# Attention and mixture of experts on one core: the first expert's products ahead of the last turns, a copy ahead of a relu, the last y on two engines

## The chip, the cores and the metric

The kernel runs on one core of one Trainium2 chip. The metric is the device time of one execution in microseconds. The core has five engines with queues of their own: TensorE (PE; its weight loads are PEld in the profile), VectorE (DVE), ScalarE (ACT), GpSimd (POOL) and SyncE (SP), which here issues most of the transfers. Matmul results stand in PSUM banks of 128 x 512 f32, everything else on the chip in SBUF.

## The reference

Causal attention with a decay for 8 batches of 8 heads (576 tokens, 64 columns per head), whose output is the input of a mixture of 8 experts with one expert per token:

```python
scores = scale * np.matmul(q, k.transpose(0, 1, 3, 2))
cum = np.cumsum(np.log(np.clip(f, 0.0001, 1.0)), axis=-1)
scores = np.where(causal, -1e9, scores + cum[:, :, :, None] - cum[:, :, None, :])
attn = softmax(scores)
x = np.matmul(attn, v)                      # 4608 tokens x 512
expert_idx = np.argmax(x @ w_gate, axis=1)  # and gate_w, its softmax value
for e in range(8):
    h = np.maximum(x[expert_idx == e] @ w1[e], 0.0)    # 512 -> 1024
    out[expert_idx == e] = gate_w * (h @ w2[e])        # 1024 -> 512
```

## The kernel before, in words

**Attention.** A loop of 34 steps handles 32 head pairs (4 per batch), each step in seven parts i = 0 to 6. In step n TensorE computes pair n's scores, VectorE adds the mask and finds the row minima (line 421), ScalarE takes the exponentials (line 428); the same step turns (transposes) pair n - 1's scores on TensorE into PSUM (line 477), ScalarE and VectorE copy them out to aT (lines 473 and 471), and in part 1 TensorE multiplies pair n - 2's turned scores with v (line 553), whose results ScalarE copies to xT (line 561). sc_03, sc_13, sc_02 and so on are the pieces of a pair's scores by head and block of rows, sc_J is the joint piece of the last 64 rows of both heads. In step 32 no scores are left to compute: only the last pair's turns, the products of pair 30, and the tasks of the batch before the last.

**Operands in two parts.** A float32 operand of a product is kept as two parts: the rounded value (a cast on ScalarE) and the rest (a subtraction on VectorE or GpSimd). Each product is done as three: first part by first part, second by first, first by second.

**The first expert starts early.** Its first 384 tokens (chunk 0, CA = 384) are taken from batches that were ready before: three blocks of 128 tokens are fetched, turned by TensorE (`turn`, line 1129), cast by ScalarE (line 1134) and completed by VectorE (line 1135, called `end` in `early_tasks`); together they are the tile xa. `up(0, 0, ft)` computes hidden block ft (of 8): for each of four blocks of w1 (kt) three products with all 384 columns of xa into one PSUM bank of the pool ps_s (three banks), then a relu on ScalarE and a rest on VectorE. `extra` calls up(0, 0, 0) to up(0, 0, 4) in parts 2 to 6 of step 32, behind the tasks of that part. Of w1's four blocks, block 1 is cast last, in part 0 of step 32 (the cast named w<-y).

**Order.** `order.pin()` keeps each engine's instructions of the attention and the first expert in the order in which the program writes them.

**Experts 1 to 7.** The first layer is computed by a scheme of seven block products in place of eight (`seven`, called four times per expert with i = 0 to 3): seven groups of six products (s = 0 to 6) into four banks a, b, g, d. Banks a, b and g are used twice: the second use (s = 4, 5, 6) adds to the first, so the copies p1 (of a, line 1422) and p5 (of g, line 1428) have to be taken in between. GpSimd adds into p5 (line 1435). A relu and a rest (line 1413 and 1416) of each of the four results follow; three of them are left for the next call, in the list `self.ends`, whose entries the next call takes in s = 0 and s = 1.

**The second layer** (`down`) sums 24 products per 128 tokens into a bank; ScalarE scales them by the gate value to y (line 1201) and GpSimd scatters y to the output (line 1202). After the last expert stands `overflow`, a loop for experts with more than 640 tokens; with these inputs its loop does not run, but the instructions ahead of it (ov_ex, ov_cm and so on) do.

Of the kernel before, what the change touches and what calls it, by code (L numbers as in the profile page):

```python
# [13 lines left out]
AF = mybir.ActivationFunctionType  # L14
ALU = mybir.AluOpType
# [4 lines left out]
P = 128  # L20
# [3 lines left out]
D = H * HD  # L24
# [17 lines left out]
HN = CAP // 2  # L42
XM = 2 * (KT // 2) * HN
XN = ("T2", "T1", "T4", "T3", "B22")


class Ctx:
# [112 lines left out]
def psum(pool):  # L160
    return pool.tile([P, 512], F32, name="ps", tag="ps")
# [10 lines left out]
    tc.nc.gpsimd.tensor_copy(c.identr, c.ident)  # L172


def attention_all(c, tc, qkT, va, vb, f, wgd, x_dram, batch_done, more_consts, extra):

# [12 lines left out]
    with ExitStack() as st:  # L191
# [534 lines left out]
        for n in range(NP + 2):  # L726
# [11 lines left out]
            for i in range(7):  # L738
# [36 lines left out]
                    step(s_)  # L775
                for f in among.pop((n, i), []):
                    step(f)
                if ts_:
                    step(ts_[i])

# [14 lines left out]
                        todo = fin_tasks(fb)  # L795

                fin_bank[0] = (ps_v, ps_m)[i % 2]
                for f in tasks.pop((n, i), []):
                    step(f)
                at = {(0, 1): 0, (1, 0): 1, (1, 1 if b == B else 4): 2}.get((p, i))  # L800
# [1 line left out]
                    fin_sums(b - 1, at)  # L802
                if (n, i) == (NP, 0):
                    scores.close()
                for f in extra(n, i):
                    step(f)
                order.pin()
                if (n, i) == (NP + 1, 1):
                    break
# [233 lines left out]
class Moe:  # L1043
    def __init__(self, c, tc, x_dram, w1, w2, out):
        self.c, self.tc, self.nc = c, tc, tc.nc
        self.x_dram, self.w1, self.w2, self.out = x_dram, w1, w2, out
        self.w1p, self.w2p, self.xg, self.x, self.h = {}, {}, {}, {}, {}
        self.idx, self.w1raw, self.w2raw, self.py = {}, {}, {}, {}

        self.ups = 5  # L1050

    def split(self, raw, w):
        self.nc.scalar.copy(w[:, 0], raw)
# [90 lines left out]
    def begin_h(self, e, chunk):  # L1144
# [4 lines left out]
            c.words["hl", chunk].rearrange("p (f n) -> p f n", n=n),  # L1149
        )  # L1150

    def up(self, e, chunk, ft):

        c, nc = self.c, self.nc
        x = self.x[e, chunk]
        hh, hl = self.h[e, chunk]
        n = (CA, CB)[chunk]
        fs = slice(ft * P, ft * P + P)
        ph = psum(c.ps_s)
        k = 0  # L1160
        for kt in range(KT):
            w = self.w1p[e, kt]
            for wi, xi in ((0, 0), (1, 0), (0, 1)):
                c.note(nc.tensor.matmul(  # L1164
                    ph[:, 0:n], w[:, wi, fs], x[xi][:, kt, :],
                    start=(k == 0), stop=(k == 3 * KT - 1),
                ))
                k += 1
        nc.scalar.activation(hh[:, ft, :], ph[:, 0:n], AF.Relu)
        nc.vector.scalar_tensor_tensor(  # L1170
            hl[:, ft, :], ph[:, 0:n], 0.0, hh[:, ft, :].bitcast(F32),
            ALU.max, ALU.subtract,
        )
# [9 lines left out]
    def down(self, e, m, part=(0, FT)):  # L1183

        c, nc = self.c, self.nc
        rows = self.rows_of_h(e, m)
        _, si, g, s = self.index(e, m)
        if part[0] == 0:
            self.py[m] = psum((c.ps_v, c.ps_m)[m % 2])
        py = self.py[m]  # L1190
        for ft in range(*part):
            w = self.w2p[e, ft]
            for k, (hi_, wi) in enumerate(((0, 0), (0, 1), (1, 0))):
                c.note(nc.tensor.matmul(  # L1194
                    py, rows(hi_, ft), w[wi],
                    start=(ft + k == 0), stop=(ft == FT - 1 and k == 2),
                ))
        if part[1] < FT:
            return
        y = c.yp.tile([P, D], F32, name="y")  # L1200
        nc.scalar.activation(y, py, AF.Copy, scale=g[:, s : s + 1])  # L1201
        nc.gpsimd.indirect_dma_start(  # L1202
            out=self.out, out_offset=bass.IndirectOffsetOnAxis(ap=si[:, s : s + 1], axis=0),
            in_=y, in_offset=None, bounds_check=self.x_dram.shape[0] - 1, oob_is_err=False,
        )
# [10 lines left out]
    def early_tasks(self):  # L1216

        c, ends = self.c, []

        def turn(m):  # L1220
            ends.append(self.turn(0, m, (c.ps_v, c.ps_m, c.ps_s)[m]))

        end = lambda: ends.pop()()
        return [(4, 1, self.early_index)] + [
            (4, 2, lambda m=m: self.fetch(0, m)) for m in range(NA)
        ] + [(5, 2, lambda: turn(0)), (5, 3, end), (5, 4, lambda: turn(1)), (5, 5, end),
             (6, 0, lambda: turn(2)), (6, 1, end)]

    def finish(self, run, t):

# [168 lines left out]
    def seven(self, e, i, run, tasks):  # L1399
# [19 lines left out]
        def after(s):  # L1419
            if s == 0:  # L1420
                self.ends.pop(0)()
                A.copy(p1, a)
                self.ends.pop(0)()
            elif s == 1:
                V.tensor_tensor(u2, b, p1, ALU.add)
# [10 lines left out]

        def end():
            relu(d, 1, 0)
            relu(p5, 1, 1)
            V.tensor_tensor(g, g, u2, ALU.add)  # L1440
            rest(d, 1, 0)

# [3 lines left out]
        for s, args in enumerate(steps):  # L1446
            run(lambda: (self.product(e, i, *args), after(s)))
            for f in tasks.get(7 * i + s, []):
                run(f)
        self.ends = [end, lambda: relu(g, 0, 1), lambda: (rest(p5, 1, 1), rest(g, 0, 1))]  # L1450

    def run(self, run, tasks):
        c, tc = self.c, self.tc
# [39 lines left out]
        with tc.tile_pool(name="moe_h", bufs=1) as hp, tc.tile_pool(name="moe_u", bufs=1) as up_, \  # L1493
# [5 lines left out]
            for e in range(1, E):  # L1499
# [33 lines left out]
                       (14, N(self.sums_s, 3)))  # L1533
                else:
                    at(ups, (27, lambda: tc.keep_in_program_order(G.drain())))
                self.ends = [lambda: None] * 3
                for i in range(FT // 2):
                    self.seven(e, i, run, ups)
                dns.setdefault(0, [])[:0] = self.ends
# [117 lines left out]
def tile_attention_moe(ctx, tc, qkT, va, vb, f, wg, w1, w2, out):  # L1657
# [22 lines left out]
    def extra(n, i):  # L1680
# [12 lines left out]
            return []  # L1693
        if i == 2:
            moe.begin_h(0, 0)
        return [lambda: moe.up(0, 0, i - 2)]

    tail = attention_all(c, tc, qkT, va, vb, f, wg, x_dram, done,
                         lambda: setup_routing(c, tc, B), extra)
    moe.run(*tail)  # L1700
    overflow(c, tc, x_dram, w1, w2, out)

# [55 lines left out]
```

## Time and profile before

| | us |
|---|---|
| median of 3 runs | 799.75 (798.74 to 800.29) |
| the profiled execution | 798.88 |
| its span, from the first to the last instruction | 797.1 |
| TensorE busy in it | 774.0 (97%) |
| VectorE / ScalarE / GpSimd busy | 581.8 / 514.8 / 541.2 |
| step 32, from the turn of sc_03 to the turn of sc_01 | 334.42 to 345.01 |
| second expert's first layer on TensorE | 409.72 to 436.21 |
| TensorE's last product ends, by the chain | 790.66 |

A row of the timeline has the start in us, the duration in us, the engine, the line, the operation, what it writes and reads, the shapes and the number of instructions merged; in brackets at the end the idle time of the engine ahead of it and what ended it. A row of the waits has who waited for whom, the sum in us, how often, and the longest. The granted clock of TensorE is 0.999 over the span.

### The profile page before, as it was taken

To read this page: it belongs to the slowest core of one execution; us is meant where nothing else is said; L and a number is where in the kernel's file an instruction comes from. 1 tells how busy PE (TensorE), PEld (TensorE's weight loads), DVE (VectorE), ACT (ScalarE), POOL (GpSimd) and SP (SyncE) were. 2 spreads that over 40 slices of the span, in tenths; PEclk is the share of its full clock that TensorE was granted. 3 is DMA by queue.
4 is the path that set the end of the run, shared out by engine and by line. 5 is a ranking of instruction groups with operands and counts; after the bars stand their busy time and mean duration, and the time that the engine had idled before them with its cause. 6 is when DMAs were issued, how large, how long until landed. Compare 5 with 4: busy or idle time off the path is not lost.

```text
span 797.1 us, 16185 instructions
## 1 busy us (share of the span) xinstructions
PE 774.0 (97%) x5496; PEld 674.4 (85%) x5496; DVE 581.8 (73%) x1654; ACT 514.8 (65%) x1278; POOL 541.2 (68%) x466
## 2 busy tenths in 40 slices
PE   4999999999999999999999999999999999999996
PEld 3888888888888888888988899898898898998985
DVE  7687989898989899756388848658488498486630
ACT  6798888888888888945456646455365365463521
POOL 6999889898989898662577657546566475475311
PEclk9999999999999999999999999999999999999999
DMA  7897787878787874533354352363343433523200
GB/s 183 220 211 181 180 195 171 193 176 196 166 202 169 202 171 135 190 100 101 118 152 147 119 170 69 112 200 96 128 130 107 154 93 107 173 69 108 105 28 31
DMA packets 66825, 114.70 MB, mean 144 GB/s; under 512 B 8295, under 2 KB 39015, under 8 KB 63412
## 3 DMA queue, kind: packets, MB, share of 16 engines
q1 hardware_dynamic: 59700, 93.71, 45.5%
q0 software_dynamic: 6400, 19.93, 7.7%
q8 instruction: 44, 0.72, 0.4%
q14 instruction: 41, 0.34, 0.1%
q10 hardware_dynamic: 640, 0.01, 0.0%
HBM read 94.05 MB, written 20.55 MB: 144 GB/s over the span
## 4 chain that ended last, share of the span: by engine, by line
PE 92%; DVE 2%; POOL 1%; ACT 1%; issue 1%; SPq 1%; DMA 1%; POOLq 0%; ACTq 0%
PE ps L1194 28%; PE ps L1393 18%; PE ps L414 17%; PE ps L553 11%; PE ps L477 10%; PE ps L1164 4%; PE pr L1393 1%; PE ps L1349 1%; PE ps L622 1%; SPq L217 1%; DMA q<-xT0w 1%; PE pr L987 1%; DVE w_1w L1308 0%; DVE hl L1416 0%; POOL u L1435 0%
## 5 line engine op out<-in xcount | busy, mean ns | idle before, releaser
L428 ACT ACTIVATE sc<-sc,nmx 128x512 f32<-128x512 f32 (+3 forms) x256 | 142.5, 559 | 10.5 <-DVE nmx L421 8.9
L421 DVE CUSTOM_DVE_ANT_0 sc<-ps,mask 128x512 f32<-128x512 f32 (+3 forms) x256 | 115.2, 485 | 33.7 <-PE ps L414 32.5
L414 PE MATMUL ps<-qk 128*128 128x288 f32 (+4 forms) x384 | 126.5, 360 | 12.2 <-ACT qk L355 10.1
L1194 PE MATMUL ps<-w_0w,hhw 128*128 128x512 f32 x280 | 112.9, 403 | 0.0
L1393 PE MATMUL ps<-X_0w,w1s 128*128 128x320 f32 x504 | 111.9, 309 | 0.0
L1194 PE MATMUL ps<-w_0w,hl 128*128 128x512 f32 x280 | 110.8, 396 | 0.0
L1194 PE MATMUL ps<-w_1w,hhw 128*128 128x512 f32 x280 | 110.3, 394 | 0.0
L414 PE MATMUL ps<-k,q 68*128 68x288 f32 (+4 forms) x384 | 107.2, 327 | 1.9 <-DMA q<-xT0w 1.9
L1202 POOL DMA_INDIRECT out<-y,si_fast x37 | 37.1, 1004 | 98.0 <-ACT y L1201 89.3
L553 PE MATMUL ps<-aT,va_t 128*64 128x256 f32 (+3 forms) x896 | 94.8, 355 | 0.0
L473 ACT COPY aT<-ps 128x512 f32<-128x512 f32 (+1 forms) x156 | 82.7, 530 | 18.5 <-PE ps L477 17.9
L330 POOL TENSOR_TENSOR qk<-raw,qk 64x1280 fp32r<-64x1280 f32 x30 | 88.2, 2939 | 2.4
L330 POOL TENSOR_TENSOR k<-raw,qk 64x1152 fp32r<-64x1152 f32 x30 | 79.7, 2656 | 10.5 <-DVE qk L373 10.5
L414 PEld LDWEIGHTS ps<-qk 128*128 128x128 f32 x384 | 70.4, 197 | 18.8 <-ACT qk L355 10.1
L1393 PEld LDWEIGHTS ps<-X_0w,w1s 128*128 128x128 f32 x504 | 84.2, 188 | 0.2
L1201 ACT ACTIVATE y<-ps,g_fast 128x512 f32<-128x512 f32 x37 | 25.5, 688 | 88.6 <-PE ps L1194 65.8
L553 PEld LDWEIGHTS ps<-aT,va_t 128*64 128x64 f32 x896 | 59.0, 137 | 26.1 <-issue 0.8
L1393 PE MATMUL ps<-X_1w,w1s 128*128 128x320 f32 x252 | 77.9, 309 | 0.0
L414 PEld LDWEIGHTS ps<-k,q 68*128 68x128 f32 x384 | 72.7, 199 | 3.1 <-POOL q L350 1.9
L1435 POOL TENSOR_TENSOR u<-u,u 128x320 f32<-128x320 f32 x28 | 24.5, 876 | 61.5 <-DVE u L1433 61.4
L1194 PEld LDWEIGHTS ps<-w_0w,hl 128*128 128x128 f32 x280 | 52.5, 187 | 12.7
L1194 PEld LDWEIGHTS ps<-w_1w,hhw 128*128 128x128 f32 x280 | 52.8, 189 | 11.1
(238 smaller groups left out, 1901.6 us busy)
## 6 DMA issues: line engine op xcount, KB each, us to landing
raw<-in_qkT SPq DMA_DIRECT2D x52, 608.0 KB
w1r<-in_w SPq DMA_DIRECT2D x112, 128.0 KB
w<-in_w SPq DMA_DIRECT2D x28, 512.0 KB
va_t<-in_va SPq DMA_DIRECT2D x32, 256.0 KB
x_dram<-row SPq DMA_DIRECT2D x32, 256.0 KB
raw<-in_qkT SPq DMA_DIRECT2D x12, 320.0 KB
wraw<-in_w SPq DMA_DIRECT2D x7, 512.0 KB
raw<-in_qkT SPq DMA_DIRECT2D x12, 288.0 KB
```

The lines of the kernel that those rows point to most:

```text
L330: return eng.tensor_tensor(o, raws[n][p0 : p0 + 64, c0:c1], ops[n][0][p0 : p0 + 64, c0:c1].bitcast(F32), ALU.subtract,)
L414: note(nc.tensor.matmul(out, ql[:, q0 : q0 + P], kl[:, j, k0 : k0 + kw], start=(i == 0), stop=(i == last),))
L421: V.tensor_tensor_reduce(dst[:, 0 : src.shape[1]], src, m, -0.125, init, ALU.add, ALU.min, nms[n][:, col : col + 1],)
L428: nc.scalar.activation(x, x, AF.Exp, bias=nms[n][:, col : col + 1], scale=-1.0, accum_out=acc)
L473: nc.scalar.copy(dst, src)
L477: note(nc.tensor.transpose(out.bitcast(F32R), words, c.identr))
L553: c.last_av = note(nc.tensor.matmul(pv[j * HD : (j + 1) * HD, q0 - qa : qb - qa], l, r, start=(blk == 0), stop=(blk == nb - 1),))
L1164: c.note(nc.tensor.matmul(ph[:, 0:n], w[:, wi, fs], x[xi][:, kt, :], start=(k == 0), stop=(k == 3 * KT - 1),))
L1194: c.note(nc.tensor.matmul(py, rows(hi_, ft), w[wi], start=(ft + k == 0), stop=(ft == FT - 1 and k == 2),))
L1201: nc.scalar.activation(y, py, AF.Copy, scale=g[:, s : s + 1])
L1202: nc.gpsimd.indirect_dma_start(out=self.out, out_offset=bass.IndirectOffsetOnAxis(ap=si[:, s : s + 1], axis=0), in_=y, in_offset=None, bou ...
L1393: self.nc.tensor.matmul(bank[:, 0:HN], w[:, wi, mat, kt], x[xi][:, kt, :], start=start and k == 0, stop=k == 5, skip_group_check=True,)
```

## The change

It has four pieces.

1. `up` is taken apart. `up_part` does the products of some blocks of w1; the order of the blocks is now 0, 3, 2, 1, so that the block that is cast last comes last. `up_first(ft)` opens a bank and does the nine products of blocks 0, 3 and 2. It is called for hidden block 0 in part 1 of step 32 ahead of that part's turn (`lead`), and for hidden block 1 in part 2; in part 3 the three remaining products of each follow. Blocks 2 to 4 stay in parts 4 to 6. In step 32 from part 2 on, `extra` stands ahead of the part's tasks instead of behind them.
2. The turn of the third x block moves from part 0 of step 32 to part 6 of step 31, and its second part from part 1 to part 0.
3. In the second expert (e = 1) ScalarE's copy p1 stands ahead of the relu of p5. For this `self.ends` has four entries instead of three; for the other experts the order stays.
4. The last y is computed in two halves, 256 columns on ScalarE and 256 on VectorE.

```diff
+W1 = (0, 3, 2, 1)
@@ attention_all, step n, part i
+                if (n, i) == (NP, 1):
+                    step(lead)
                 if ts_:
                     step(ts_[i])
...
+                if n == NP and i > 1:
+                    for f in extra(n, i):
+                        step(f)
                 for f in tasks.pop((n, i), []):
                     step(f)
...
-                for f in extra(n, i):
-                    step(f)
+                if n != NP or i < 2:
+                    for f in extra(n, i):
+                        step(f)
@@ class Moe
+    def up_part(self, e, chunk, ft, ph, kts):
+        c, x = self.c, self.x[e, chunk]
+        for kt in kts:
+            w = self.w1p[e, kt]
+            for k, (wi, xi) in enumerate(((0, 0), (1, 0), (0, 1))):
+                c.note(self.nc.tensor.matmul(
+                    ph[:, 0 : (CA, CB)[chunk]], w[:, wi, ft * P : ft * P + P], x[xi][:, kt, :],
+                    start=(kt == W1[0] and k == 0), stop=(kt == W1[-1] and k == 2),
+                ))
+
+    def up_first(self, ft):
+        self.ph[ft] = psum(self.c.ps_s)
+        self.up_part(0, 0, ft, self.ph[ft], W1[:3])
+
     def up(self, e, chunk, ft):
...
+        ph = self.ph.pop(ft, None)
+        if ph is None:
+            ph = psum(c.ps_s)
+            self.up_part(e, chunk, ft, ph, W1)
+        else:
+            self.up_part(e, chunk, ft, ph, W1[3:])
@@ down
-        nc.scalar.activation(y, py, AF.Copy, scale=g[:, s : s + 1])
+        if (e, m) == (E - 1, NST - 1):
+            nc.scalar.activation(y[:, 0 : D // 2], py[:, 0 : D // 2], AF.Copy,
+                                 scale=g[:, s : s + 1])
+            nc.vector.tensor_scalar(y[:, D // 2 :], py[:, D // 2 :], g[:, s : s + 1], None,
+                                    ALU.mult)
+        else:
+            nc.scalar.activation(y, py, AF.Copy, scale=g[:, s : s + 1])
@@ early_tasks
-             (6, 0, lambda: turn(2)), (6, 1, end)]
+             (5, 6, lambda: turn(2)), (6, 0, end)]
@@ seven, after s = 0
                 self.ends.pop(0)()
+                if e > 1:
+                    self.ends.pop(0)()
                 A.copy(p1, a)
+                if e == 1:
+                    self.ends.pop(0)()
                 self.ends.pop(0)()
...
         def end():
             relu(d, 1, 0)
-            relu(p5, 1, 1)
...
-        self.ends = [end, lambda: relu(g, 0, 1), lambda: (rest(p5, 1, 1), rest(g, 0, 1))]
+        self.ends = [end, lambda: relu(p5, 1, 1), lambda: relu(g, 0, 1),
+                     lambda: (rest(p5, 1, 1), rest(g, 0, 1))]
@@ extra, step 32
         if i == 2:
             moe.begin_h(0, 0)
-        return [lambda: moe.up(0, 0, i - 2)]
+            return [lambda: moe.up_first(1)]
+        return [lambda ft=ft: moe.up(0, 0, ft) for ft in ((0, 1) if i == 3 else (i - 2,))]
```

The order on TensorE in the last pair's turns, from the turn of sc_J on (line 477 turns, line 1129 turns an x block, line 553 multiplies with v, w_4831, w_5179, w_4998 and w_4955 are w1's blocks 0, 1, 2 and 3). Before:

```order
L477 MATMUL ps<-identr,sc_Jw 128x128 x4
L477 MATMUL ps<-identr,sc_03w 128x128 x4
L1129 MATMUL ps<-identr,xg 128x128 x4
L477 MATMUL ps<-identr,sc_13w 128x128 x4
L553 MATMUL ps<-aT_91,va_t 64x256 x6
...
L477 MATMUL ps<-identr,sc_02w 128x128 x4
L477 MATMUL ps<-identr,xT1w 128x128 x4
L1164 MATMUL ps<-xa,w_4831 128x384 x3
L1164 MATMUL ps<-xa,w_5179 128x384 x3
L1164 MATMUL ps<-xa,w_4998 128x384 x3
L1164 MATMUL ps<-xa,w_4955 128x384 x3
L477 MATMUL ps<-identr,sc_12w 128x128 x4
```

Now (the same lines have the numbers 479, 1137, 555 and 1166; w1's block 1 is w_5180):

```order
L479 MATMUL ps<-identr,sc_Jw 128x128 x4
L1137 MATMUL ps<-identr,xg 128x128 x4
L479 MATMUL ps<-identr,sc_03w 128x128 x4
L1166 MATMUL ps<-xa,w_4831 128x384 x3
L1166 MATMUL ps<-xa,w_4955 128x384 x3
L1166 MATMUL ps<-xa,w_4998 128x384 x3
L479 MATMUL ps<-identr,sc_13w 128x128 x4
...
L479 MATMUL ps<-identr,sc_02w 128x128 x4
...
L479 MATMUL ps<-identr,xT1w 128x128 x4
L479 MATMUL ps<-identr,sc_12w 128x128 x4
L1166 MATMUL ps<-xa,w_5180 128x384 x6
```

The third x block is turned ahead of sc_03, and nine products stand between the turns of sc_03 and sc_13, where none stood; nine more stand between the turns of sc_02 and xT (not shown), and the six of block 1 behind the turn of sc_12.

ScalarE at the same place, from the last exponential on. Before:

```order
L428 ACTIVATE sc_J,jsum<-sc_J,nmx 128x576
L473 COPY aT_97<-ps 128x4x128
L1134 CAST xa<-ps 128x4x128
L1053 CAST w_5179<-y 128x512 x2
L473 COPY aT_97<-ps 128x4x128
```

Now:

```order
L430 ACTIVATE sc_J,jsum<-sc_J,nmx 128x576
L1142 CAST xa<-ps 128x4x128
L475 COPY aT_97<-ps 128x4x128
L1061 CAST w_5180<-y 128x512 x2
L475 COPY aT_97<-ps 128x4x128
```

The cast of the third x block and the copy of the turned sc_03 have changed places; both still stand behind the exponential of sc_J.

ScalarE in the second expert, around the start of the second call of `seven` (u_6060 is the first call's p5, u_6132 the second call's p1, u_6133 its p5). Before:

```order
L1413 ACTIVATE hhw<-ps 128x320
L1413 ACTIVATE hhw<-u_6060 128x320
L1422 COPY u_6132<-ps 128x320
L1413 ACTIVATE hhw<-ps 128x320
L1292 CAST w1s<-w1r 128x1024
L1428 COPY u_6133<-ps 128x320
```

Now:

```order
L1437 ACTIVATE hhw<-ps 128x320
L1448 COPY u_6132<-ps 128x320
L1437 ACTIVATE hhw<-u_6060 128x320
L1437 ACTIVATE hhw<-ps 128x320
L1316 CAST w1s<-w1r 128x1024
L1456 COPY u_6133<-ps 128x320
```

The copy p1 and the relu of p5 have changed places, in the second, third and fourth call; nothing else on ScalarE moves there, and VectorE's order is the same as before.

VectorE at the end of the program, now:

```order
L1582 TENSOR_SCALAR ov_ex<-rk 128x8
L1589 MEMSET ov_one 128x8
L1597 MEMSET ov_cnt 128x1
L1585 TENSOR_TENSOR ov_cm<-ov_ex,iotaP 128x288
L1222 TENSOR_SCALAR y<-ps,g_fast 128x256
L1587 TENSOR_REDUCE ov_ex<-ov_cm 128x8
```

VectorE's half of the last y stands behind the first instructions of `overflow`; the row of y is the only new one. In the built program it waits for ScalarE's half, and GpSimd's scatter waits for it.

More of the change, by code (lines that the diff above doesn't have):

```diff
@@ L172, in setup_consts, with attention_all @@
     tc.nc.gpsimd.tensor_copy(c.identr, c.ident)
-def attention_all(c, tc, qkT, va, vb, f, wgd, x_dram, batch_done, more_consts, extra):
+def attention_all(c, tc, qkT, va, vb, f, wgd, x_dram, batch_done, more_consts, extra, lead):
     nc = tc.nc
@@ L1048, in __init__ @@
         self.idx, self.w1raw, self.w2raw, self.py = {}, {}, {}, {}
-        self.ups = 5
+        self.ph = {}
     def split(self, raw, w):
@@ L1150, in begin_h @@
         )
+    def up_part(self, e, chunk, ft, ph, kts):
[10 more added lines that the diff above has]
+        self.up_part(0, 0, ft, self.ph[ft], W1[:3])
     def up(self, e, chunk, ft):
         c, nc = self.c, self.nc
-        x = self.x[e, chunk]
         hh, hl = self.h[e, chunk]
         n = (CA, CB)[chunk]
[L1158 to L1168, printed above, removed]
+        ph = self.ph.pop(ft, None)
[4 more added lines that the diff above has]
+            self.up_part(e, chunk, ft, ph, W1[3:])
         nc.scalar.activation(hh[:, ft, :], ph[:, 0:n], AF.Relu)
@@ L1535, in run @@
                     at(ups, (27, lambda: tc.keep_in_program_order(G.drain())))
-                self.ends = [lambda: None] * 3
+                self.ends = [lambda: None] * 4
                 for i in range(FT // 2):
@@ L1695, in extra @@
             moe.begin_h(0, 0)
-        return [lambda: moe.up(0, 0, i - 2)]
+            return [lambda: moe.up_first(1)]
+        return [lambda ft=ft: moe.up(0, 0, ft) for ft in ((0, 1) if i == 3 else (i - 2,))]
     tail = attention_all(c, tc, qkT, va, vb, f, wg, x_dram, done,
-                         lambda: setup_routing(c, tc, B), extra)
+                         lambda: setup_routing(c, tc, B), extra, lambda: moe.up_first(0))
     moe.run(*tail)
```

## The prediction

> **What bounds the kernel now.** I read the page first: the busy line, then the chain that ended last.
>
> ```profile
> span 797.1 us, 16185 instructions
> PE 92%; DVE 2%; POOL 1%; ACT 1%; issue 1%; SPq 1%; DMA 1%; POOLq 0%; ACTq 0%
> ```
>
> TensorE is 92% of the chain. No other engine sets the end, so a microsecond counts where TensorE stands still, and any new wait of TensorE counts in full. Hence the second view, the waits, for TensorE alone. These are all its waits after the start of the program:
>
> ```profile
> PE ps L1393 <- ACT u L1422: 0.9, 3, 0.4
> PE ps L477 <- ACT xT L561: 0.5, 1, 0.5
> PE ps L477 <- DVE aT L471: 0.5, 1, 0.5
> PE ps L477 <- ACT aT L473: 0.3, 1, 0.3
> ```
>
> The three of line 477 are in the last pair's turns (step 32 of the attention loop); the one of line 1393 is in the second expert (e = 1). Together 2.2 us: that is what the first two parts of the change can win by this view. The third part is the end of the program.
>
> **Part 1: the last pair's turns.** TensorE's timeline there, before:
>
> ```profile
> 333.47 0.46 PE L477 MATMUL ps<-identr,sc_Jw 128*128 128x128 f32 x4
> 334.42 0.53 PE L477 MATMUL ps<-identr,sc_03w 128*128 128x128 f32 x4 [0.49 <-DVE aT L471]
> 334.80 0.51 PE L1129 MATMUL ps<-identr,xg 128*128 128x128 f32 x4
> 335.61 0.54 PE L477 MATMUL ps<-identr,sc_13w 128*128 128x128 f32 x4 [0.31 <-ACT aT L473]
> ...
> 340.00 0.53 PE L477 MATMUL ps<-identr,xT1w 128*128 128x128 f32 x4 [0.53 <-ACT xT L561]
> 340.37 2.33 PE L1164 MATMUL ps<-xa,w 128*128 128x384 f32 x12
> 342.54 0.46 PE L477 MATMUL ps<-identr,sc_12w 128*128 128x128 f32 x4
> ...
> 345.01 0.28 PE L477 MATMUL ps<-identr,sc_01w 128*128 128x128 f32 x2
> ```
>
> The change puts the turn of the third x block (line 1129) right behind the first row, and nine products of hidden block 0 ahead of the turn of sc_13. Those nine read all 384 columns of xa, so they need the third block's first part, written by ScalarE's cast, and its second part, written by VectorE. When are these ready? The rows of ScalarE and VectorE, before:
>
> ```profile
> 336.33 0.78 ACT L428 ACTIVATE sc_J<-sc_J,nmx 128x576 f32<-128x576 f32 x1 [0.77 <-DVE nmx L421]
> 337.10 0.56 ACT L473 COPY aT<-ps 128x512 f32<-128x512 f32 x1
> 337.57 0.58 ACT L1134 CAST xa<-ps 128x512 fp32r<-128x512 f32 x1
> ...
> 338.19 0.69 DVE L1135 TENSOR_TENSOR xa<-ps,xa 128x512 fp32r<-128x512 f32 x1 [1.95 <-ACT xa L1134]
> ```
>
> The order rows show the cast one place earlier, but still behind the exponential of sc_J, and that one waited 0.77 us for VectorE's minimum, which the change does not touch. So the cast starts at 337.10 in place of 337.57, ends at 337.10 + 0.58 = 337.68, and VectorE's part runs from 337.72 to 338.41.
>
> TensorE is at the nine much earlier. The third block's turn fills a part of the 0.49 us wait; sc_03 still waits for VectorE's copy until 334.42 and is done about 334.8. Then TensorE stands until 337.73: a new wait of about 2.9 us, where before it did sc_13's turn and 2.87 us of attention products. Two products later it waits again until 338.45 for the second part.
>
> Now the sum to a common point, the turn of sc_01. One product takes (342.54 - 340.37) / 12 = 0.181 us, nine 1.63. After the second wait seven remain, 1.27; with about 0.2 us for two restarts (the turn of sc_13, restarted after a wait, took 0.47 to its successor, a turn without wait about 0.3) sc_13 is at 338.45 + 1.27 + 0.2 = 339.9. Before it was at 335.61: 4.3 us later. From there to sc_01 took 345.01 - 335.61 = 9.40 us before. Of that the change saves 1.63 (nine products are done), 0.70 (the wait at 340.00, by its spacing: ScalarE's copies of xT now have the other nine products of block 1 as cover), and some 0.2 of restarts: 6.9. So sc_01 is at 346.8, **+1.75 us**. Bounds: +1.5 if restarts are free and the second wait is shorter, +2.1 if none of the restarts is saved. That nothing behind it gives this back I take from the waits: from 345 to the second expert TensorE has no wait that a later arrival could shorten.
>
> What is moved along: the products of blocks 2 to 4 stand ahead of the turns of xT, the load of two w2 pieces ahead of the write of x rows on the SP queue, a w2 split ahead of Rr on GpSimd. Rr is then done around 352.4, its reader (line 987 before) at 354.8; the turn that needs VectorE's copy of sc_01 comes at 352.1, the copy by my count at 350.3. I cost these at nothing; the cover is 2 us each, and 0.5 us if it is gone.
>
> **Part 2: the copy ahead of the relu, e = 1.** TensorE by the first product of each group of six, and ScalarE's and VectorE's rows in the first of the three waits:
>
> ```profile
> 409.72 1.04 PE L1393 MATMUL ps<-xa,w1s 128*128 128x320 f32 x6
> 415.89 1.04 PE L1393 MATMUL ps<-xa,w1s 128*128 128x320 f32 x6
> 420.00 1.14 PE L1393 MATMUL ps<-xa,w1s 128*128 128x320 f32 x6 [0.44 <-ACT u L1422]
> 421.86 0.55 PE L1393 MATMUL ps<-X_0w,w1s 128*128 128x320 f32 x2
> 422.84 1.04 PE L1393 MATMUL ps<-xa,w1s 128*128 128x320 f32 x6
> 429.58 1.04 PE L1393 MATMUL ps<-xa,w1s 128*128 128x320 f32 x6
> 436.21 0.39 PE L1194 MATMUL ps<-w_0w,hhw 128*128 128x512 f32 x1
> ```
>
> ```profile
> 416.55 0.44 ACT L1413 ACTIVATE hhw<-ps 128x320 fp32r<-128x320 f32 x1 [1.00 <-DVE ps L1434]
> 419.16 0.47 ACT L1413 ACTIVATE hhw<-u 128x320 fp32r<-128x320 f32 x1 [2.18 <-POOL u L1435]
> 419.54 0.41 ACT L1422 COPY u<-ps 128x320 f32<-128x320 f32 x1
> 420.17 1.05 ACT L1292 CAST w1s<-w1r 128x1024 fp32r<-128x1024 f32 x1
> 421.38 0.43 ACT L1428 COPY u<-ps 128x320 f32<-128x320 f32 x1 [0.15 <-DVE hl L1416]
> ...
> 420.39 0.88 DVE L1416 SCALAR_TENSOR_TENSOR hl<-u,hhw 128x320 fp32r<-128x320 f32 x1
> ```
>
> A group of seven blocks without a wait takes 415.89 - 409.72 = 6.17 us. The next three take 6.95, 6.74 and 6.63 (differences of the rows): 0.78, 0.57 and 0.46 over, **1.81 us** in all. The waits view names 0.9 of it; the rest are restarts and the stretched row at 421.86. With the copy of line 1422 right behind the relu at 416.55 it ends about 417.3, and TensorE needs it at 419.4: that wait is gone. But the relu of p5 still starts at 419.16, since it waits for GpSimd; then VectorE's row of 0.88 (earlier now, 419.66 to 420.5), the relu, the cast of 1.05, and only about 420.85 to 421.3 the copy of line 1428, which the last six products wait for. They would arrive at 415.89 + 36 x 6.17 / 42 = 421.2. So 0.1 to 0.2 us stay in each of the three, some 0.5 in all. I take **-1.3 us**; bounds -0.9 (only the named waits) and -1.8 (all).
>
> **Part 3: the last y.** VectorE, ScalarE and GpSimd at the end, and the nearest rows for half a tile:
>
> ```profile
> 790.73 0.69 ACT L1201 ACTIVATE y<-ps,g_fast 128x512 f32<-128x512 f32 x1 [4.91 <-PE ps L1194]
> 790.89 0.46 DVE L1557 TENSOR_TENSOR ov_cm<-ov_ex,iotaP 128x288 f32<-128x288 f32 x1
> 791.69 0.97 POOL L1202 DMA_INDIRECT out<-y,si_fast  x1 [4.63 <-ACT y L1201]
> ...
> 355.66 0.37 ACT L561 COPY xT<-ps 128x256 f32<-128x256 f32 x1 [1.94 <-PE ps L553]
> ...
> 333.00 0.41 DVE L421 CUSTOM_DVE_ANT_0 sc<-ps,mask 128x256 f32<-128x256 f32 x1
> ```
>
> Side by side the halves would end near 791.15 in place of 791.42. But VectorE's half stands behind ov_cm, which ends at 791.35, and in the built program it waits for ScalarE's half of the same tile. So it runs from about 791.35 to 791.75, and the scatter, 0.27 us behind its input as before, starts near 792.05 in place of 791.69: **+0.35 us**. Bounds: -0.3 (side by side after all), +0.6 (the four waits put ahead of it each cost time).
>
> **Sum.** 1.75 - 1.3 + 0.35 = +0.8 us. The profiled execution took 798.88 us (797.1 of span and 1.8 around it): 799.7. It lies 0.87 under the median of the three runs, 799.75; I forecast against the median: **800.5 us**. Own range, from the bounds and the spread of 1.6 us in the three runs: 799.0 to 802.0.
>
> **The rivals.** *The first nine products do not wait* (the change does what it says). For it: the wait at 334.42 to 335.61 and the one at 340.00 lose 2.0 us by spacing, and filling them is worth that. Then -2.0 - 1.3 + 0.35, 796.8 us. Against it: the cast's place behind the exponential. 10%.
>
> *The copy only hands the wait on.* If GpSimd's p5 or the slow VectorE row of 0.88 comes as late as now relative to TensorE, the last six products of each group wait in its place, and of -1.3 some -0.1 is left: +2.0, 801.8 us, slower. For it: the relu of p5 at 419.16 does not move; against it: VectorE's row can start 0.7 earlier. 14%.
>
> *TensorE comes back slow from the new wait.* The trace has a slow pace at the start, after an idle of 10.11 us:
>
> ```profile
> 10.11 0.79 PE L414 MATMUL ps<-qk 128*128 128x512 f32 x1 [10.11 <-ACT qk L355]
> 31.58 0.76 PE L414 MATMUL ps<-qk 128*128 128x512 f32 x1
> 41.11 0.47 PE L414 MATMUL ps<-qk 128*128 128x512 f32 x1
> ```
>
> The same product takes 1.6 times as long, for over 21 us. If a pause of 2.9 us brought this on, 5 us of work at that pace cost 3 us more: about 803.5 us, slower; all of 21 us would cost over 10. Against it: pauses of 0.5 us left the pace unchanged at 340, and none near 3 us stands in the busy part of this trace. It decides from the length at which a pause slows the engine, which I can't read here. 8%. The Trainium skill ("TensorE: Matmul & The Clock Gate", "Why this matters for your kernels") advises no idle gap of TensorE over about 3 us, since a whole idle window brings half clock back; by that rule 2.9 us is just under the edge. No row of before shows that edge.
>
> **How the numbers follow.** The forecast case has 66%, the three rivals 10, 14 and 8, 2 are left for what I have not seen. A measurement of this kernel tells about 0.2%, 1.6 us, from no change. The forecast case lies within it but for its upper end (5 of the 66). So faster 12, same 61, slower 27. The range of 8 in 10 takes the forecast's own range and the middle rival: 798.9 to 802.2.
>
> **What would show it.** Right: TensorE's largest wait is a new one of 2.5 to 3.2 us, by the products of expert 0's first layer on the cast of xa; the waits on xT and on u are gone from its list; the second expert's seven-block groups take about 6.3 us; the last scatter starts 1.3 to 1.4 us behind TensorE's end (1.0 before). Wrong: no wait at the nine, or the groups at 6.6 or more, or these products spaced 0.25 us and more after 338 (0.181 before).

## The result, and the profile after

| | before | after |
|---|---|---|
| median in us (lowest to highest) | 799.33 (798.72 to 800.29) | 804.32 (803.15 to 805.28) |
| the profiled execution | 798.88 | 805.28 |
| its span | 797.1 | 803.5 |

The ratio after to before is 1.0055, with a 95% interval from 1.0046 to 1.0065: the change costs 5 us, where 0.8 had been forecast. The two profiled executions differ by 6.40 us, 1.4 more than the medians: the profiled one of after is the slowest of its six.

TensorE's waits after the first 70 us, in the waits of after (who waited for whom; sum in us, how often, the longest):

```profile
PE ps L1166 <- ACT xa L1142: 2.8, 1, 2.8
PE ps L555 <- issue: 1.0, 1, 1.0
PE ps L1417 <- ACT u L1456: 0.7, 2, 0.4
PE ps L1373 <- DMA xg<-x_dram,gi_fast: 0.7, 1, 0.7
PE ps L1137 <- DMA xg<-x_dram,gi_fast: 0.4, 1, 0.4
```

The first is the new wait that was forecast at about 2.9 us, on the cast of the third x block. The second, "issue" ahead of the last pair's products with v, was not forecast. The third is what stays in the second expert. The last two are waits on gathered x rows. The waits of before have none; the traces of the experiments below have such a wait with 0.2 to 0.4 us, the one of the kernel that changes only the last y among them. They are not followed here.

TensorE's timeline of after, from the turn of sc_J to the last pair's products with v:

```profile
333.64 0.46 PE L479 MATMUL ps<-identr,sc_Jw 128*128 128x128 f32 x4
333.96 0.54 PE L1137 MATMUL ps<-identr,xg 128*128 128x128 f32 x4
334.56 0.53 PE L479 MATMUL ps<-identr,sc_03w 128*128 128x128 f32 x4
337.86 3.33 PE L1166 MATMUL ps<-xa,w 128*128 128x384 f32 x9 [2.77 <-ACT xa L1142]
340.99 0.67 PE L479 MATMUL ps<-identr,sc_13w 128*128 128x128 f32 x4
...
345.79 1.81 PE L1166 MATMUL ps<-xa,w 128*128 128x384 f32 x9
...
349.21 0.29 PE L479 MATMUL ps<-identr,sc_01w 128*128 128x128 f32 x2
...
358.98 1.84 PE L555 MATMUL ps<-aT,va_t 128*64 128x256 f32 x16 [1.04 <-issue]
```

Nine products take 3.33 us behind the pause; the next nine, of the same shape, take 1.81. From the turn of sc_J to the turn of sc_01 it is 15.57 us, where before it was 345.01 - 333.47 = 11.54: 4.03 us more, not 1.75. A view by stretches says why. Its columns are the stretch, its length, the busy time of TensorE, its weight loads, VectorE, ScalarE and GpSimd, then the granted clock, the DMA share and GB/s. The stretches are cut where the granted clock changes, and 3.41 us apart:

```profile
333.34:336.75 3.41, 1.69 (x16) 1.41 (x14) 2.86 (x11) 2.33 (x7) 0.00 (x0) 1.00 0.63 219
336.75:340.17 3.42, 2.31 (x7) 2.09 (x8) 2.06 (x10) 2.58 (x6) 1.28 (x2) 0.50 0.01 2
340.17:343.58 3.41, 3.41 (x18) 2.44 (x18) 0.93 (x7) 0.59 (x1) 1.23 (x2) 0.50 0.00 0
343.58:346.00 2.42, 2.42 (x29) 1.83 (x28) 0.00 (x0) 0.80 (x2) 0.00 (x0) 1.00 0.00 0
```

TensorE stands from 335.09 to 337.86. The granted clock falls to 0.50 inside this pause, at 336.75, and stays there for 6.83 us, until 343.58. So TensorE works 5.7 us at half clock.

The 1.04 us at 358.98 has this around it (after, TensorE and VectorE):

```profile
357.01 0.41 PE L479 MATMUL ps<-identr,xT1w 128*64 128x128 f32 x4
357.25 0.69 PE L995 MATMUL pr<-Rr,Ar 128*128 128x240 bf16 x5
357.73 0.56 DVE L1188 SCALAR_TENSOR_TENSOR hl0w<-ps,hh0w 128x384 fp32r<-128x384 f32 x1 [1.64 <-ACT hh0w L1187]
358.20 0.67 DVE L600 TENSOR_TENSOR row<-ps,rinv 64x512 f32<-64x512 f32 x1
```

TensorE's products follow 0.11 us behind the end of VectorE's row of line 600 (358.20 + 0.67 = 358.87). That row empties the bank into which the last x row was turned at 357.01, and the last pair's first products with v are written to the same bank: `fin_bank[0] = (ps_v, ps_m)[i % 2]` in part 6, and `zip(AV, (ps_v, ps_m))` in the products. Before the change twelve products (2.3 us) stood between that turn and these products; now they stand ahead of the turn. VectorE's row is late because it stands behind the rest of the same hidden block (line 1188), which waits for ScalarE's relu of these twelve products. The list of waits calls this "issue"; it is an instruction of its own, in the queue of the weight loads. The view of line 555 has it, from 355.5 on for 3455 ns, that is until 358.95:

```profile
L555 PEldq EVENT_SEMAPHORE  x1: 3455/3455/3455, 355.5 to 355.5; - x1
```

The second expert in after:

```profile
416.20 1.04 PE L1417 MATMUL ps<-xa,w1s 128*128 128x320 f32 x6
422.37 1.04 PE L1417 MATMUL ps<-xa,w1s 128*128 128x320 f32 x6
428.23 0.56 PE L1417 MATMUL ps<-X_0w,w1s 128*128 128x320 f32 x2 [0.43 <-ACT u L1456]
429.21 1.04 PE L1417 MATMUL ps<-xa,w1s 128*128 128x320 f32 x6
434.95 0.56 PE L1417 MATMUL ps<-X_0w,w1s 128*128 128x320 f32 x2 [0.30 <-ACT u L1456]
435.94 1.04 PE L1417 MATMUL ps<-xa,w1s 128*128 128x320 f32 x6
442.23 0.39 PE L1212 MATMUL ps<-w_0w,hhw 128*128 128x512 f32 x1
```

The groups of seven blocks take 6.17, 6.84, 6.73 and 6.29 us (before 6.17, 6.95, 6.74 and 6.63): 0.46 us gained, where 1.3 was forecast. The wait is still there, now on the copy of p5 (line 1456). One trace of before makes this look better than it is: two kernels below that keep the old order in this expert take 26.22 and 26.28 us in all, where before takes 26.49 and after 26.03. Against them after gains 0.2 to 0.3.

The end of after:

```profile
796.31 0.40 PE L1212 MATMUL ps<-w_0w,hl 128*128 128x512 f32 x1
796.95 0.46 DVE L1585 TENSOR_TENSOR ov_cm<-ov_ex,iotaP 128x288 f32<-128x288 f32 x1
797.35 0.49 DVE L1222 TENSOR_SCALAR y<-ps,g_fast 128x256 f32<-128x256 f32 x1
798.12 0.97 POOL L1226 DMA_INDIRECT out<-y,si_fast  x1 [4.99 <-DVE y L1222]
```

The last scatter starts 1.41 us behind TensorE's end (796.71); before it was 791.69 - 790.66 = 1.03. That is +0.38, as forecast (0.35).

The terms add up to 4.03 + 1.04 - 0.46 + 0.38 = 4.99 us. They are read from the two profiled executions, which differ by 6.40; most of the rest is a start that was 0.17 later and the waits on gathered rows (0.7 and 0.4). That the medians differ by 4.99 as well is chance: the half clock is worth less in the other traces with this pause, as the first experiment shows. The mean granted clock is 0.994 in the profiled execution and 0.996 or 0.997 in the other five, so the long slow stretch is probably this execution's own.

### The profile page after: what moved, and what is told of

Read it like the earlier page. It is cut to its first block, busy times and chain, and to the rows that moved or that the text cites. A ratio compares the mean times of both kernels' runs of the same rounds, so it can differ in the third digit from the quotient of the medians.

```text
span 803.5 us, 16190 instructions
## 1 busy us (share of the span) xinstructions
PE 775.9 (97%) x5496; PEld 676.4 (84%) x5496; DVE 584.2 (73%) x1655; ACT 515.4 (64%) x1278; POOL 542.2 (67%) x466
## 4 chain that ended last, share of the span: by engine, by line
PE 88%; DMA 3%; issue 2%; DVE 2%; POOL 2%; SPq 1%; ACT 1%; DVEq 0%; POOLq 0%; ACTq 0%
PE ps L1212 27%; PE ps L1417 19%; PE ps L416 15%; PE ps L555 11%; PE ps L479 9%; PE ps L1166 3%; PE pr L1417 1%; SPq L219 1%; PE ps L1373 1%; PE ps L624 1%; DMA k<-ck 1%; DMA raw<-in_qkT 1%; DMA xg<-x_dram,gi_fast 1%; DMA q<-xT0w 1%; PE pr L995 1%
```

## The experiments

**Each part alone.** The first kernel has pieces 1 and 2 of the change, with the second expert and the last y as before (the diff is against the changed kernel, in `seven` and `down`).

```diff
-                if e > 1:
-                    self.ends.pop(0)()
+                self.ends.pop(0)()
                 A.copy(p1, a)
-                if e == 1:
-                    self.ends.pop(0)()
...
-        if (e, m) == (E - 1, NST - 1):
-            nc.scalar.activation(y[:, 0 : D // 2], py[:, 0 : D // 2], AF.Copy,
...
+        nc.scalar.activation(y, py, AF.Copy, scale=g[:, s : s + 1])
```

> The kernel before with the first two pieces alone (products ahead, third x block's turn earlier). If the loss is theirs: 804.3 + 0.5 - 0.4 = 804.4 us, with the wait of 2.8 us, the clock of 0.5 and the 1 us gap ahead of the last attention products as in the changed kernel. If the pieces act on each other, it is under 803 or over 806.

Measured: 804.07 us, ratio 1.0053 (1.0031 to 1.0075): nearly the whole loss stands here. Pause, half clock and the gap at line 555 are there again:

```profile
333.20:336.61 3.41, 2.49 (x22) 2.17 (x20) 3.24 (x12) 2.81 (x10) 0.00 (x0) 1.00 0.84 301
336.61:340.02 3.41, 1.38 (x6) 1.06 (x7) 1.81 (x8) 2.86 (x6) 0.46 (x1) 1.00 0.02 4
340.02:343.44 3.42, 3.42 (x19) 2.45 (x19) 1.61 (x11) 0.59 (x1) 2.06 (x2) 0.50 0.00 0
```

(view by stretches, as above.) But the clock falls at another moment. The pause lasts from 335.77 to 338.53; the clock falls at 340.02, 1.5 us after it has ended, and for 3.41 us in place of 6.83. From sc_J to sc_01 it is 14.85 us here, 0.7 less than in after. By the rows this kernel loses 14.85 - 11.54 + 1.04 = 4.35 us, by the medians of its set 4.57. With pieces 3 and 4 (-0.2 to -0.5 and +0.38) that makes 4.2 to 4.5 us for the whole change, within the interval of its ratio (3.7 to 5.2 us).

The second kernel has piece 3 alone (against the kernel before, in `seven`).

```diff
+                if e > 1:
+                    self.ends.pop(0)()
                 A.copy(p1, a)
+                if e == 1:
+                    self.ends.pop(0)()
...
-            relu(p5, 1, 1)
...
+        self.ends = [end, lambda: relu(p5, 1, 1), lambda: relu(g, 0, 1),
+                     lambda: (rest(p5, 1, 1), rest(g, 0, 1))]
```

> The kernel before with the copy ahead of the relu alone. By the prediction -1.3 us: 798.0, groups of seven blocks of about 6.3 us. By the trace of the changed kernel -0.5 us: 798.8, groups of 6.84, 6.73 and 6.29 us, and TensorE waits for the copy of p5 (0.7 us in all) in place of the copy of p1.

Measured: 799.24 us, ratio 0.9993 (0.9983 to 1.0002). Its groups take 6.17, 6.68, 6.73 and 6.29 us, 0.62 less in all than before and 0.4 less than the two other traces with the old order; TensorE waits on the copy of p5 as in after. That is a gain of about half a microsecond, which its interval does not tell from nothing.

The third has piece 4 alone (against the kernel before, in `down`).

```diff
-        nc.scalar.activation(y, py, AF.Copy, scale=g[:, s : s + 1])
+        if (e, m) == (E - 1, NST - 1):
+            nc.scalar.activation(y[:, 0 : D // 2], py[:, 0 : D // 2], AF.Copy,
+                                 scale=g[:, s : s + 1])
+            nc.vector.tensor_scalar(y[:, D // 2 :], py[:, D // 2 :], g[:, s : s + 1], None,
+                                    ALU.mult)
+        else:
+            nc.scalar.activation(y, py, AF.Copy, scale=g[:, s : s + 1])
```

> The kernel before with the last y by two engines alone. By the prediction and the trace of the changed kernel +0.35 us: 799.7, the last scatter starts 1.40 us behind TensorE's end in place of 1.03. If the halves ran side by side: -0.3 us, the scatter 0.7 to 0.8 behind.

Measured: 799.56 us, ratio 1.0002 (0.9990 to 1.0014). In its trace TensorE ends at 791.22 and the scatter starts at 792.63: 1.41 us as in after, against 1.03. The time alone can't show this; the rows do.

**Is it the clock?** The pause ahead of the first nine products is filled with products whose result nobody reads; nothing is left out. They are added to the changed kernel ahead of the first nine:

```diff
+        if ft == 0:
+            pad = psum(self.c.ps_v)
+            for _ in range(12):
+                self.c.note(self.nc.tensor.matmul(
+                    pad, self.c.identr, self.w1p[0, 0][:, 0, 0:512], start=True, stop=True))
```

> The changed kernel, with 12 products of 512 columns (identity by a ready w1 block, into a bank that is read by nobody) put ahead of the first nine products, so that TensorE has 2.8 us of work where the change makes it stand. Nothing else differs, and the nine products can start no earlier. Theory 'slow pace' (the pause of 2.77 us halves the granted clock until about 343): no clock under 0.95 between 334 and 346, the nine products take about 1.8 us in place of 3.33, the turn of sc_01 comes about 2.3 us earlier than in the changed kernel, the whole about 802.0 us. Theory 'wait alone' (the rest of the loss comes from the moved order or from transfers): the nine products keep their 3.3 us or the loss shows elsewhere, the whole stays at 804.3.

Measured: 802.79 us, ratio 1.0038 (1.0027 to 1.0049), with work added. Its timeline, and the clock by the view by stretches:

```profile
334.70 0.46 PE L479 MATMUL ps<-identr,sc_Jw 128*128 128x128 f32 x4
336.02 3.03 PE L1176 MATMUL ps<-w,identr 128*128 128x512 f32 x12
338.96 2.23 PE L1166 MATMUL ps<-xa,w 128*128 128x384 f32 x9
348.08 0.29 PE L479 MATMUL ps<-identr,sc_01w 128*128 128x128 f32 x2
```

```profile
330.00:346.00 16.00, 15.82 (x128) 13.57 (x128) 9.26 (x41) 11.65 (x33) 5.97 (x4) 1.00 0.27 97
```

The turns and the cast keep their order, and the nine start 4.26 us behind sc_J (4.22 in after), but there is no pause: the clock stays at 1.00, the nine take 2.23 in place of 3.33, and sc_J to sc_01 is 13.38 us in place of 15.57. What is left, 13.38 - 11.54 = +1.84, is the wait by itself, forecast at +1.75. The other 2.2 us are the half clock in the profiled execution of after. By the times it is less, 804.32 to 802.79 or 0.0017 of the ratio, and the two intervals overlap a little; the expectation had 802.0. That fits the 1.3 to 1.5 us that the half clock costs where it lasts 3.41 us, as in the kernel with pieces 1 and 2 alone (14.85 - 13.38).

**How long may the pause be?** The same with six and with three added products (`range(6)`, `range(3)`).

> The changed kernel with 6 in place of 12 products (512 columns, results read by nobody) ahead of the first nine; they add work to the computation and leave nothing out. Six of them took half of 3.03 us, so TensorE's wait ahead of the nine should be about 1.3 us. Clock-gate theory with an edge near 3 us or between 1.3 and 2.8: granted clock 1.0 over 334 to 346, the twelve... nine products at 0.20 to 0.25 each, turn of sc_Jw to turn of sc_01 about 13.4 us. If any pause of a microsecond brings half clock: granted clock under 0.9 somewhere in 337 to 346, and 14.5 us or more. By either the issue gap of 1.04 us ahead of the last pair's products with v is there.

> The same with 3 added products: a wait of about 2.0 us. If the pause that slows TensorE has its edge above 2.0: granted clock 1.0, sc_Jw to sc_01 about 13.4 us. If the edge lies between 1.3 and 2.0: granted clock about 0.5 for some 5 us, 15.3 us or so. A proportional effect (a longer pause, a longer slow stretch) would show a slow stretch shorter than the 5.4 us behind the 2.77 us pause.

The pause and what follows, with six (first fence) and with three (second), by stretches:

```profile
335.40:338.81 3.41, 2.10 (x12) 1.43 (x10) 1.77 (x7) 2.64 (x7) 0.00 (x0) 1.00 0.21 78
338.81:342.22 3.41, 3.30 (x25) 2.53 (x25) 2.60 (x15) 1.68 (x4) 2.52 (x2) 1.00 0.00 0
```

```profile
335.49:338.90 3.41, 1.41 (x9) 0.87 (x7) 1.77 (x7) 2.64 (x7) 0.00 (x0) 1.00 0.19 70
338.90:342.31 3.41, 3.40 (x15) 2.84 (x13) 2.60 (x15) 1.11 (x3) 2.51 (x2) 0.50 0.00 0
342.31:345.00 2.69, 2.69 (x33) 1.89 (x32) 0.00 (x0) 0.96 (x2) 0.00 (x0) 1.00 0.00 0
```

A pause of 1.31 us leaves the clock alone (sc_J to sc_01 13.34 us); one of 2.01 us, which ends at 338.54, brings half clock from 338.90 to 342.31 (14.65 us; expected were some 5 us of it and 15.3). One execution of each was timed, 803.07 and 804.39 us. So a pause well under the 2.77 us of the change is enough, and well under the 3 us of which I had written that 2.9 was "just under the edge".

The stretches are cut at 3.41 us for a reason. Each trace keeps the moments at which the granted clock changes. In all twelve traces the distance between any two of them is a whole number of steps of 3.413 us: 3.41, 6.83, 303.79 (89 steps), 457.39 (134), 761.17 (223). And in these pauses the clock of a step follows how long TensorE stood in the step before:

- In after the pause lies across a border. The step up to 336.75 has 3.41 - 1.69 = 1.72 us of standing, and the clock falls; the next, at half clock, has 1.10 us, and the clock stays low; the third has none, and the clock comes back. Hence two slow steps.
- With pieces 1 and 2 alone the two steps have 0.92 and 2.03 us. Only behind the second does the clock fall, and then TensorE has long been at work again. Hence one slow step, 1.5 us behind the pause.
- With three added products it is 2.00 us and one slow step, with six 1.31 us and none.

The end of the program, where TensorE has no more work, shows the same in the traces of the order as before (first fence, the next experiment) and of the twelve added products (second): 3.41 - 1.51 = 1.90 us of standing leave the next step at 1.00, and 3.41 - 1.46 = 1.95 bring 0.50.

```profile
793.53:796.94 3.41, 1.51 (x7) 0.89 (x5) 1.78 (x9) 0.47 (x1) 0.49 (x1) 1.00 0.00 0
796.94:800.35 3.41, 0.00 (x0) 0.00 (x0) 0.05 (x1) 0.00 (x0) 0.48 (x1) 1.00 0.09 27
```

```profile
793.26:796.67 3.41, 1.46 (x7) 0.83 (x5) 1.83 (x9) 0.47 (x1) 0.54 (x1) 1.00 0.00 0
796.67:800.00 3.33, 0.00 (x0) 0.00 (x0) 0.00 (x0) 0.00 (x0) 0.43 (x1) 0.50 0.09 28
```

So the edge is about half a step, but not one figure of standing time: between 1.31 and 1.72 us in the last pair's turns, between 1.90 and 1.95 behind the last products. Why the two differ is open.

**Where does the gap at line 555 come from?** The changed kernel, with the first expert's products behind the part's tasks again from part 2 on, as before.

```diff
-                if n == NP and i > 1:
-                    for f in extra(n, i):
-                        step(f)
                 for f in tasks.pop((n, i), []):
                     step(f)
...
-                if n != NP or i < 2:
-                    for f in extra(n, i):
-                        step(f)
+                for f in extra(n, i):
+                    step(f)
```

> The changed kernel, but from part 2 of step 32 on the products of the first expert stand behind the tasks of the part, as before; so SyncE's queue and GpSimd's have the order of before (the write of x rows ahead of the load of two w2 pieces). The pause ahead of the first nine and the half clock stay by every theory. If the issue gap of 1.04 us ahead of the last pair's products with v comes from the moved order of transfers and of GpSimd's work: no such gap, and about 803.3. If it comes from elsewhere (the place of the program in which TensorE stands, its late arrival): the gap stays, and about 804.3.

Measured: 803.39 us, ratio 1.0044 (1.0031 to 1.0057). The pause of 2.76 us is there, with one slow step behind it (339.55 to 342.96; sc_J to sc_01 14.83 us). The gap is gone (TensorE's timeline, and VectorE's row):

```profile
354.86 0.41 PE L479 MATMUL ps<-identr,xT1w 128*64 128x128 f32 x4
355.11 2.30 PE L1162 MATMUL ps<-xa,w 128*128 128x384 f32 x12
357.25 0.69 PE L991 MATMUL pr<-Rr,Ar 128*128 128x240 bf16 x5
357.86 1.84 PE L555 MATMUL ps<-aT,va_t 128*64 128x256 f32 x16
```

```profile
355.76 0.67 DVE L600 TENSOR_TENSOR row<-ps,rinv 64x512 f32<-64x512 f32 x1
```

The expectation had named the order of transfers and GpSimd's work as the cause. The rows say more simply: the twelve products stand behind the turn again, VectorE's row ends at 356.43, and the bank is free 1.4 us before TensorE wants it. I had looked at busy transfers because the DMA share was 0.91 from 356 to 358 in after; but in the gap itself, from 357.94 to 358.98, it is 0.10, and in all six traces that have the gap TensorE starts 0.10 or 0.11 us behind VectorE's row (354.05 + 0.67 = 354.72 and 354.83 in the next kernel). That transfers play no part was not tried by itself.

**The products without the pause.** The changed kernel with the first nine products behind the products of pair 30 with v.

```diff
-                if (n, i) == (NP, 1):
-                    step(lead)
                 if ts_:
                     step(ts_[i])
...
                     step(lambda: av(n - 2))
                     av_out()
+                    if n == NP:
+                        step(lead)
```

> The changed kernel, but the first nine products stand behind the products of pair 30 with v of part 1 in place of ahead of the turn of sc_13; all else as changed. Theory (the loss is TensorE's pause and the clock behind it): no wait over 1 us at the nine, granted clock 1.0, the turn of sc_01 at about 344.4 (0.6 to 0.8 us ahead of before); with -0.46 of the second expert and +0.37 at the end 798.5 to 798.9 where the issue gap of 1.04 us goes too, 799.5 to 799.9 where it stays. Rival (products split over the turns cost time by themselves, such as turns and products alternating): 801 or more at full clock.

Measured: 800.16 us, ratio 1.0002 (0.9990 to 1.0013). No wait over 0.7 us there, clock 1.00, sc_J to sc_01 345.02 - 334.17 = 10.85 us, 0.69 less than before. The gap of 1.04 us is there, as in all kernels with the new order; with +0.38 at the end this eats the gain. (Expected with the gap: 799.5 to 799.9.)

Then both cures together (this edit and that of the order), with the last y on ScalarE alone:

```diff
-        if (e, m) == (E - 1, NST - 1):
-            nc.scalar.activation(y[:, 0 : D // 2], py[:, 0 : D // 2], AF.Copy,
...
+        nc.scalar.activation(y, py, AF.Copy, scale=g[:, s : s + 1])
```

> The changed kernel with the first nine products behind the products of pair 30 with v (as in the run with the late lead), the products of the first expert from part 2 on behind the tasks of their part (as in the run with the order as before), and the last y on ScalarE alone as before. Theory (pause, clock and late x row together make the whole loss): no pause over 0.7 us, granted clock 1.0, no gap ahead of the last pair's products with v; sc_Jw to sc_01 10.9 us in place of 11.54 (-0.7), the second expert -0.5, the end as before: -1.2, ratio 0.9985. Rival (the x rows or the transfers cost the same elsewhere): ratio 0.9995 or more.

Measured: 798.78 us, ratio 0.9989 (0.9980 to 0.9998); sc_J to sc_01 10.87 us, no gap, second expert 25.85 us in place of 26.49.

**What holds the second expert?** That kernel, with one word changed in the second expert: the sum into p5 on VectorE.

```diff
-            G.tensor_tensor(p5, u3, p5, ALU.add)
+            (V if e == 1 else G).tensor_tensor(p5, u3, p5, ALU.add)
```

> The run before it in this set, and in the second expert the sum into p5 on VectorE in place of GpSimd. If the wait left in the second expert is the late p5 (GpSimd's sum, then the relu, VectorE's rest and only then the copy that TensorE waits for): the relu of p5 starts about 1.3 us earlier, no wait of TensorE on u stays, the first seven-block groups take 6.2 to 6.3 us each in place of 6.2 to 6.8, and 0.7 to 0.9 us are gained over the other run. If VectorE or ScalarE is itself the bound there: groups as before, within 0.2 us of the other run.

Measured: 797.19 us, ratio 0.9976 (0.9964 to 0.9988). The groups take 6.17, 6.14, 6.38 and 6.34 us, 25.03 in all (before 26.49): 0.82 less than the kernel beside it, as expected, and no wait on u. Against before that is 1.46 us, and 1.2 against the two other traces with the old order: what the forecast had put at 1.3. (The medians of the two kernels differ by 1.6 us; their intervals overlap, and the rows show 0.82 of it.) The relu of p5 did start earlier, but the rows of VectorE and GpSimd show that this is not the whole of it. First after, then this kernel:

```profile
425.44 1.87 POOL L1322 TENSOR_TENSOR w1s<-w1r,w1s 128x768 fp32r<-128x768 f32 x1
426.03 1.63 DVE L1440 SCALAR_TENSOR_TENSOR hl<-u,hhw 128x320 fp32r<-128x320 f32 x1 [1.16 <-ACT hhw L1437]
```

```profile
418.39 1.86 POOL L1312 TENSOR_TENSOR w1s<-w1r,w1s 128x768 fp32r<-128x768 f32 x1
418.47 2.13 DVE L1430 SCALAR_TENSOR_TENSOR hl<-u,hhw 128x320 fp32r<-128x320 f32 x1
```

VectorE's rest of p5 ends at 427.66, 0.35 us behind GpSimd's split of w1 (427.31). In the other kernel it starts in the shadow of the same split and ends at 420.60, again 0.35 behind it (420.25); and in the rows of before, 421.27 against 419.09 + 1.83 = 420.92, again 0.35. The last of these rows in after, with no such split beside it, takes 0.48. So it is GpSimd's split, not its own start, that ends VectorE's row: measured from the group's start (415.89 before, 422.37 after) it begins 0.84 us earlier in after, and it takes 0.75 us longer. With GpSimd's sum out of the way the split itself starts earlier in the group, 2.33 us behind its start, where in after it is 3.07.

The Trainium skill ("SBUF — State Buffer", "SBUF: two separate sides") has this as a rule: an operation of VectorE with two inputs from SBUF and one of GpSimd take a shared port as an exclusive lock, and the loser waits for the whole instruction. The three ends at 0.35 us agree with it. So do rows of VectorE that read one of their inputs from PSUM: in before two of them (425.84 and 426.71) take 0.49 us each beside the split of 425.82 to 427.66.

## Why the prediction was wrong

- **Part 1, the wait itself: right.** The wait of 2.77 us on the cast was forecast at 2.9, and the loss up to sc_01 without the clock is 1.80 to 1.84 us in the filled kernels, forecast 1.75. The place behind the exponential was read from the rows, and that reading held.
- **Part 1, the clock: the step that failed.** The sum put the pause at its own length, and the half clock behind it at 8% as the third rival, since "2.9 us is just under the edge". It happened, at 2.2 us in the profiled execution and 1.3 to 1.5 in three others (sc_J to sc_01 14.65 to 14.85 against 13.3). The rival's own price (803.5 us) was nearer to the result than the forecast. What made it look unlikely was the length: no row of before showed how long a pause has to be, and 2.01 us were enough. Its evidence, the slow products from 10 to 32 us, was better than it looked. The view prints 1.00 there, and over all of before 0.999, but the clock's records begin only at 34.76 us in before (32.97 to 36.24 in the twelve traces); ahead of that there is none. The pace changes at that very moment: in before a 128x256 product with v takes 0.63 us at 34.07 and 0.38 at 34.84. So the slow start looks like the same half clock, without a record of its own.
- **Part 1, "I cost these at nothing; the cover is 2 us each, and 0.5 us if it is gone": the second step that failed, +1.04 us.** Rr and the copy of sc_01 were looked at, and no wait of TensorE on either stands in after. VectorE's multiplication of the last x row was not looked at: the edit moved twelve products from behind its turn to ahead of it, and the bank that it empties was wanted at once.
- **Part 2: half right, and a term mis-sized (-0.46 for -1.3, and -0.2 to -0.5 over the traces).** The copy of p1 goes early and its wait is gone. The step that failed was "then VectorE's row of 0.88 (earlier now, 419.66 to 420.5)": it started earlier and took 1.63, so the copy of p5 came late. This is the second rival, in part: the wait was handed on, with a loss of 0.8 us or more against the forecast.
- **Part 3: right** (+0.38 for +0.35).
- **"What would show it"** named the slow spacing: 0.25 us and more after 338. The nine products are spaced 3.13 / 9 = 0.35 us. Of the signs for the forecast, the wait on the cast came; the wait on u stayed, and two of the three groups took over 6.6 us.

What stays open: what exactly a step of 3.41 us counts. The standing time by the rows orders the steps of the last pair's turns and those of the program's end, but with another edge in each. The start does not fit at all: in before TensorE is busy for 14.47 of the 14.76 us ahead of 34.76, and the pace stays slow until then. Where the borders of the steps fall is another matter in each trace (the first change stands at 32.97 to 36.24 us): nearly the same pause cost one slow step in two kernels and two in after. The Trainium skill ("TensorE: Matmul & The Clock Gate", "What's actually happening") describes such a free-running window of 3.4 us; the lengths agree with it. Its half clock "after ≥1 idle window" does not agree, if that is a window without work: here 1.72 to 2.03 us of standing in a window were enough.

## What to carry to other kernels

A new pause on the engine that sets the end is not priced at its length: in these runs one of 2.0 to 2.8 us cost 1.3 to 2.2 us more at half clock. So work that waits for a late operand goes behind work that is ready: behind the attention products the same nine gained 0.7 us in the turns, where they had lost 4. When products move past a turn, look up every reader of every bank that the turn fills: what stood behind it was its cover. And a row that starts earlier does not end earlier if it shares something with another engine's row; look where its stretched instances end.

## What was not expected of the hardware

- A pause of TensorE of 2.01 us brought a granted clock of 0.50; one of 1.31 us did not. The clock changed in steps of 3.413 us only, and behind these pauses a step's clock followed the standing time of the step before, so it can fall up to 1.5 us after the pause, when the engine is busy again.
- The view's granted clock of 1.00 in the first 33 to 36 us is no record: the clock's records begin there, at the moment at which the pace rises.
- VectorE's row of 0.48 us took 0.88, 1.63 and 2.13 us beside GpSimd's split of 1.85, and ended 0.35 us behind it each time.
- "Issue" in the list of waits can be a wait on another engine: here on VectorE's row of line 600, which ends 0.11 us ahead of TensorE's start.
